# Norms four tiles ahead, Q of chunk 0 before K(4), and weight loads regrouped over two queues, in a linear-attention plus SwiGLU block

## The chip, the cores and the metric

The kernel runs on one core of a Trainium2 chip. Times are device microseconds (us) of one execution. A time in the tables is the median of a kernel's runs; the span of a profile, from its first to its last instruction, is about 1.7 us shorter than the time of the same execution. "Profile" and "trace" are the hardware profiler's record of one execution.

The engines are called as the profile calls them: PE is TensorE (matmuls), PEld its weight loads, DVE VectorE, ACT ScalarE, POOL GpSimd, SP SyncE. The kernel runs alone, so there is no second core to disturb it. A run more than 1.5% above the fastest of its kernel in the batch is counted as slow, and ratios leave it out.

## The reference, cut to what matters

```python
x = A_x                                   # 1 x 2048 x 512, bf16
xn = _layernorm(x, axis=-1)
return x + _A_ref(xn, A_wqkv, A_wo) + _B_ref(xn, B_w_gate, B_w_up, B_w_down)

# _A_ref: linear attention, 32 heads of 16
phi = lambda t: jnp.where(t > 0, t + 1, jnp.exp(t)) + 1e-6
pq, pk = phi(q), phi(k)
kv  = einsum("bhsd,bhse->bhde", pk, v);  z = einsum("bhsd->bhd", pk)
o   = einsum("bhqd,bhde->bhqe", pq, kv) / (einsum("bhqd,bhd->bhq", pq, z)[..., None] + 1e-6)
# _B_ref: (silu(xn @ w_gate) * (xn @ w_up)) @ w_down, inner width 1792
```

## The kernel before: the parts that matter

There are 16 tiles of 128 rows of x. For each tile t: VectorE computes the statistics (`bn1`, `bn2`), ScalarE the reciprocal root (`rs`: Ln, then Exp), and VectorE (tiles 0 to 3) or GpSimd (tiles 4 to 15) normalises. The normalised tile must be transposed. Tiles 0 to 3 go through PE and an eviction; the others go through a DMA transpose issued on the SyncE queue. Then PE computes K(t) of the tile, Q products (`qproj(i)`, four for each chunk of four tiles), and the accumulation `gacc(t)`. Every K or Q product ends in a chain over one of four PSUM banks (`phi`): exp on ScalarE, min on GpSimd, max-and-add on VectorE. This is the first stage, up to about 53 us. After it come 56 pairs of gate and up products, with the rest of the attention between them.

Each engine runs its own list in program order. A program-order list means that an instruction that is ready can still stand behind one that is not.

```python
        K.add("act", lambda e: e.preload_act_table_set("natural_log_exp_and_others"))
        xload("sp", 0)
        xload("act", 1)
        wload("sp", 1)          # K weights, 512 KB
        xload("act", 2)
        xload("sp", 3)
        xload("act", 4)
        wload("sp", 0)          # Q weights
        ...
        def norm(t):
            bn1(t)
            bn2(t)
            rs(t)
            lna_pool(t)
            dmat(t)             # DMA transpose, SyncE queue
            for piece in PIECES[t]:
                piece()         # weight loads of 448 to 896 KB, behind the transpose of tile 6, 7, ... 15
        ...
        for s in range(4, NT + 2):
            ends = []
            if s < NT:
                ends.append(kproj(s))
            for i in SQ[s]:
                ends.append(qproj(i))
            gacc(s - 2)
            if s + 3 < NT:
                norm(s + 3)     # three tiles ahead
            for e_ in ends:
                e_()
```

## Time and profile before

| | before |
|---|---|
| time, median of the first 3 runs | 224.49 us |
| span of the profiled execution | 222.1 us |
| PE busy | 213.5 us (96%) |
| end of the fourth K product (start of the first Q product) | 12.93 us |
| first gate matmul | 53.04 us |

The page of the profile gives busy time and count for each engine, a digit of busy tenths for each fortieth of the span, and the share of each engine in the chain of work that ended last. These are three of its lines from the kernel before.

```profile
PE 213.5 (96%) x1063; PEld 96.6 (43%) x1063; DVE 101.5 (46%) x171; ACT 70.2 (32%) x138; POOL 35.9 (16%) x81
...
PE   7599979999999999999999999999999999999995
...
PE 90%; ACT 3%; DMA 3%; DVE 2%; issue 0%; POOL 0%
```

PE is the limit, and its gaps are in the first third. The timeline of PE shows them one by one. Columns: start us, duration us, engine, source line, operation, tiles, count, and in brackets the idle time before it with what ended it. L219 is the warm-up (matmuls on zeros), L255 the PE transposes, L293 the K products, L302 the Q products, L309 `gacc`, L396 the gate and up products, L429 the z sum.

```profile
1.26 4.02 PE L219 MATMUL pb<-warm 128*128 128x512 bf16 x9 [1.26 <-DVE warm L197]
5.33 0.61 PE L255 MATMUL pb<-ident,xn 128*128 128x128 bf16 x4
7.06 0.40 PE L255 MATMUL pb<-ident,xn 128*128 128x128 bf16 x4 [1.13 <-DVE xn L237]
7.30 1.03 PE L293 MATMUL pb<-wqkv,xnT 128*128 128x512 bf16 x4
...
12.93 1.89 PE L302 MATMUL pb<-xnT,wqkv 128*128 128x512 bf16 x8
...
23.95 1.02 PE L293 MATMUL pb<-wqkv,xnT 128*128 128x512 bf16 x4 [0.50 <-DMA xnT<-xn]
...
33.19 1.02 PE L293 MATMUL pb<-wqkv,xnT 128*128 128x512 bf16 x4 [1.31 <-DVE pqT L287]
...
53.04 1.03 PE L396 MATMUL pb<-xnT,wg 128*128 128x512 bf16 x4
...
55.42 1.05 PE L429 MATMUL pb<-pk,ones 128*32 128x512 bf16 x16 [0.49 <-ACT GT L412]
```

Two things are to be read here. A group of four 128x512 matmuls takes 1.03 us in this view, with the drain of the last one; the next group starts 0.864 us after it, which is 0.216 us a matmul. The wait before K(10), at 33.19 us, is put down to VectorE, but VectorE had long freed the bank (at 29.62 us, after K(8)); the DMA transpose of tile 10, issued at 28.22 us, took 4.8 us to land, and this fits the start of K(10).

### The profile page before, as it was taken

What the parts mean: (1) busy time and instruction counts of PE and PEld (TensorE: products, weight loads), DVE (VectorE), ACT (ScalarE), POOL (GpSimd) and SP (SyncE); (2) the same over time, 40 slices, a digit from 0 to 9 for tenths busy, and PEclk for the clock granted to TensorE, in tenths of its full rate; (3) what the DMA queues carried; (4) which work ended last, traced back from release to release, by engine and by line L of the source; (5) the groups of instructions that cost most, each with busy time, mean ns of one, the idle gap of its engine ahead of it and who ended that gap; (6) DMA issues with size and microseconds to landing.
All of it is one profiled execution on the core that took longest, in us unless ns stands there. A gap on an engine that the chain in (4) does not pass through costs nothing.

```text
span 222.1 us, 2756 instructions
## 1 busy us (share of the span) xinstructions
PE 213.5 (96%) x1063; PEld 96.6 (43%) x1063; DVE 101.5 (46%) x171; ACT 70.2 (32%) x138; POOL 35.9 (16%) x81
## 2 busy tenths in 40 slices
PE   7599979999999999999999999999999999999995
PEld 2244334443544444444444444444444444444454
DVE  4598786655566777723223232422424232232121
ACT  3675555767372233313102131311313220130000
POOL 4187785843022000000000000000000000000000
DMA  6915999894000000000000000000000000000101
GB/s 204 351 36 134 255 183 234 224 270 152 0 0 3 0 0 0 3 0 24 24 0 27 24 0 0 24 24 2 25 24 0 3 24 0 25 24 3 47 24 47
DMA packets 16381, 13.55 MB, mean 61 GB/s; under 512 B 7280, under 2 KB 15344, under 8 KB 16368
## 3 DMA queue, kind: packets, MB, share of 16 engines
q1 hardware_dynamic: 15792, 12.85, 20.7%
q10 hardware_dynamic: 576, 0.52, 0.7%
q8 instruction: 8, 0.13, 0.3%
q14 instruction: 5, 0.04, 0.1%
HBM read 9.70 MB, written 2.10 MB: 53 GB/s over the span
## 4 chain that ended last, share of the span: by engine, by line
PE 90%; ACT 3%; DMA 3%; DVE 2%; issue 0%; POOL 0%
PE pb L396 43%; PE pb L492 22%; PE pb L488 6%; PE pb L302 6%; PE pb L293 5%; PE pb L309 5%; DMA xnT<-xn 1%; DMA x_sb<-in_A_x_dram 1%; PE pb L475 1%; ACT ef L283 1%; DVE xn L237 1%; PE pb L255 1%; ACT xnT L262 1%; ACT L400 1%; DVE stats L224 1%
## 5 line engine op out<-in xcount | busy, mean ns | idle before, releaser
L400 ACT ACTIVATE sil<-pb 128x512 bf16<-128x512 f32 x56 | 33.4, 597 | 106.0 <-PE pb L396 100.2
L405 DVE TENSOR_TENSOR hT<-pb,sil 128x512 bf16<-128x512 f32 x56 | 38.6, 688 | 46.9 <-PE pb L396 46.9
L396 PE MATMUL pb<-xnT,wg 128*128 128x512 bf16 x224 | 57.6, 379 | 0.0
L396 PE MATMUL pb<-xnT,wu 128*128 128x512 bf16 x224 | 57.5, 379 | 0.0
L492 PE MATMUL pb<-wd,hT 128*128 128x512 bf16 (+1 forms) x238 | 51.2, 366 | 0.0
L492 PEld LDWEIGHTS pb<-wd,hT 128*128 128x128 bf16 x238 | 23.3, 98 | 25.1
L498 DVE TENSOR_TENSOR out_sb<-pb,x_sb 128x512 bf16<-128x512 f32 (+1 forms) x17 | 11.2, 661 | 49.9 <-PE pb L492 49.9
L396 PEld LDWEIGHTS pb<-xnT,wu 128*128 128x128 bf16 x224 | 21.9, 98 | 26.4
L396 PEld LDWEIGHTS pb<-xnT,wg 128*128 128x128 bf16 x224 | 21.4, 98 | 27.3 <-issue 2.5
L283 ACT ACTIVATE ef<-pb 128x512 bf16<-128x512 f32 x32 | 19.0, 595 | 15.0 <-PE pb L293 9.9
L284 POOL TENSOR_SCALAR ef<-ef 128x512 bf16<-128x512 bf16 x32 | 19.6, 614 | 17.3 <-ACT ef L283 16.7
L293 PE MATMUL pb<-wqkv,xnT 128*128 128x512 bf16 x64 | 16.3, 379 | 1.8 <-DVE pqT L287 1.3
L488 PE MATMUL pb<-M,pqT 128*128 128x512 bf16 (+1 forms) x68 | 16.6, 366 | 0.0
L309 PE MATMUL pb<-pk,xn 128*128 128x512 bf16 x64 | 16.3, 379 | 0.0
L302 PE MATMUL pb<-xnT,wqkv 128*128 128x512 bf16 x64 | 16.1, 379 | 0.0
L287 DVE SCALAR_TENSOR_TENSOR pk<-pb,ef 128x512 bf16<-128x512 f32 x16 | 11.0, 686 | 7.8 <-POOL ef L284 7.8
L287 DVE SCALAR_TENSOR_TENSOR pqT<-pb,ef 128x512 bf16<-128x512 f32 x16 | 11.0, 691 | 4.2 <-POOL ef L284 4.1
L224 DVE BATCH_NORM_STATS2 stats<-x_sb 128x6 f32<-128x512 bf16 x16 | 10.9, 682 | 2.1 <-DMA x_sb<-in_A_x_dram 2.1
L483 DVE TENSOR_TENSOR pqT<-pb,pqT 128x512 bf16<-128x512 f32 x16 | 10.6, 681 | 0.0
L293 PEld LDWEIGHTS pb<-wqkv,xnT 128*128 128x128 bf16 x64 | 5.9, 98 | 9.2 <-DVE pqT L287 1.8
L488 PEld LDWEIGHTS pb<-M,pqT 128*128 128x128 bf16 x68 | 6.7, 98 | 7.4
L245 POOL TENSOR_SCALAR xn<-x_sb,nm,rstd 128x512 bf16<-128x512 bf16 x12 | 9.3, 772 | 2.0 <-ACT rstd L233 1.0
(61 smaller groups left out, 72.5 us busy)
## 6 DMA issues: line engine op xcount, KB each, us to landing
out_dram<-out_sb SPq DMA_DIRECT2D x15, 128.0 KB, 1.7
wg<-in_B_w_gate_dram SPq DMA_DIRECT2D x4, 448.0 KB, 5.1
wu<-in_B_w_up_dram SPq DMA_DIRECT2D x4, 448.0 KB, 3.8
wd<-in_B_w_down_dram SPq DMA_DIRECT2D x2, 896.0 KB, 7.4
x_sb<-in_A_x_dram SPq DMA_DIRECT2D x12, 128.0 KB, 5.1
wqkv<-in_A_wqkv_dram SPq DMA_DIRECT2D x3, 512.0 KB, 4.4
x_sb<-in_A_x_dram ACTq DMA_DIRECT2D x4, 128.0 KB, 4.5
wo<-in_A_wo_dram SPq DMA_DIRECT2D x1, 512.0 KB, 3.8
```

The source lines that it names most:

```text
L224: K.add("dve", lambda e: e.bn_stats(stats[:, t, :], x_sb[:, t, :]), r=[("x", t)], w=[("st", t)])
L283: K.add("act", lambda e: e.activation(buf, banks[b][:, :], ACT.Exp), r=[B(b)], w=[bkey])
L284: K.add("pool", lambda e: e.tensor_scalar(out=buf, in0=buf, scalar1=1.0 + 1e-6, scalar2=0.0, op0=ALU.min, op1=ALU.max), r=[bkey], w=[bkey])
L287: return lambda: K.add("dve", lambda e: e.scalar_tensor_tensor(out=dst, in0=banks[b][:, :], scalar=1e-6, in1=buf, op0=ALU.max, op1=ALU.add ...
L293: K.add("pe", [(lambda e, c=c: e.matmul(banks[b][:, :], xnT[:, c, t * P:(t + 1) * P], wqkv[:, c, D:2 * D], start=(c == 0), stop=(c == NDC ...
L302: K.add("pe", [(lambda e, c=c: e.matmul(banks[b][:, :], wqkv[:, c, g * P:(g + 1) * P], xnT[:, c, C * 512:(C + 1) * 512], start=(c == 0), s ...
L309: K.add("pe", [(lambda e, c=c: e.matmul(banks[c][:, :], xn[:, t, c * P:(c + 1) * P], pk[:, t, :], start=(t == 0), stop=(t == NT - 1))) for ...
L396: K.add("pe", [(lambda e, c=c, b=b, w_=w_: e.matmul(banks[b][:, :], w_[:, c, fc * P:(fc + 1) * P], xnT[:, c, C * 512:(C + 1) * 512], start ...
L400: K.add("act", lambda e: e.activation(sil[:, j % 2, :], banks[gb(j)][:, :], ACT.Silu), r=[B(gb(j))], w=[("sil", j % 2)])
L405: K.add("dve", lambda e: e.tensor_tensor(out=hT[:, C % 2, fc, :], in0=banks[gb(j) + 1][:, :], in1=sil[:, j % 2, :], op=ALU.mult), r=[B(gb( ...
L488: fns = [(lambda e, g=g: e.matmul(banks[bank][:, 0:hi - lo], pqT[:, g, t * P:(t + 1) * P], M[:, g, lo:hi], start=(g == 0), stop=False)) fo ...
L492: fns = [(lambda e, fc=fc: e.matmul(banks[bank][:, 0:hi - lo], hT[:, C % 2, fc, jj * P:(jj + 1) * P], wd[:, fc, lo:hi], start=False, stop= ...
```

## The change

The intent is to close those gaps. It has six parts:

1. x(0) is loaded in two column halves, one on each queue. x(1) thereby becomes the second load on the scalar queue.
2. K products run between the transposes, and evictions on ScalarE come ahead of exps.
3. The four Q products of chunk 0 come before K(4), and norms run four tiles ahead.
4. The first halves of the gate and up weights, the V weights and the output weights are loaded from the scalar queue between exps.
5. The second halves of gate and up, and the down weights, are loaded behind the last transpose.
6. The evictions of the G accumulators come ahead of the first silu, the z sum follows the second gate/up pair, and the denominator moves from after pair 2 to after pair 4 (the pairs are counted from 0).

The diff, cut to its core:

```diff
-        xload("sp", 0)
+        for h, eng in ((0, "sp"), (1, "act")):
+            load(eng, ("x", 0, h), x_sb[:, 0, h * 256:h * 256 + 256], xin[0:P, h * 256:h * 256 + 256])
         xload("act", 1)
         wload("sp", 1)
...
-        transp(0, 0, 0, 2)
-        transp(0, 1, 2, 4)
-        evac(0, 0, "act", 0, 2)
+        transp(0, 0)
         bn2(1)
-        evac(0, 1, "dve", 2, 4)
         rs(1)
-        lna_dve(1)
-        transp(1, 2)
-        evac(1, 2)
+        evac(0, 0)
         bn1(2)
         bn2(2)
         rs(2)
-        k0 = kproj(0)
+        lna_dve(1)
+        transp(1, 1)
+        evac(1, 1)
...
         norm(5)
+        k0()
+        q0 = qproj(0)
         k1()
-        q0 = qproj(0)
+        norm(6)
+        q1 = qproj(1)
         k2()
-        q1 = qproj(1)
+        k3()
         gacc(0)
...
+        AL = {4: lambda: fload("act", "wg", wg, B_w_gate, 0), 6: lambda: fload("act", "wu", wu, B_w_up, 0),
+              8: lambda: wload("act", 2), 10: lambda: woload("act")}
         for s in range(4, NT + 2):
...
-            if s + 3 < NT:
-                norm(s + 3)
+            if s + 4 < NT:
+                norm(s + 4)
+            if s in AL:
+                AL[s]()
...
+        for h in (1,):
+            fload("sp", "wg", wg, B_w_gate, h)
+            fload("sp", "wu", wu, B_w_up, h)
+        for lo in WD_LO:
+            dload("sp", lo)
...
+            elif j == 4:
+                den_mm()
+                hop(j)
+                recip(0)
+                recip(1)
+            elif j == 5:
+                hop(j)
                 recip(2)
                 recip(3)
-            elif j in (6, 9, 12, 15):
-                g = (j - 6) // 3
+            elif j in (7, 10, 13, 16):
+                g = (j - 7) // 3
                 bc_mm(g)
```

More of the change, by code (lines that the diff above doesn't have):

```diff
@@ L169, in wload, with woload, fload, dload @@
                  A_wqkv[:, i * D:(i + 1) * D].rearrange("(c p) f -> p c f", p=P))
-        def rload(key, dst, src, lo, hi):
-            load("sp", (key, lo), dst[:, lo:hi, :], src[lo * P:hi * P, :].rearrange("(c p) f -> p c f", p=P))
-        WD_LO = (0, 7)
-        PIECES = {t: [] for t in range(4, NT)}
-        PIECES[6].append(lambda: wload("sp", 2))
-        PIECES[7].append(lambda: rload("wo", wo, A_wo, 0, 4))
-        for c in range(NDC):
-            PIECES[8 + c].append(lambda c=c: rload("wg", wg, B_w_gate, c, c + 1))
-            PIECES[12 + c].append(lambda c=c: rload("wu", wu, B_w_up, c, c + 1))
-        for lo in WD_LO:
-            PIECES[15].append(lambda lo=lo: rload("wd", wd, B_w_down, lo, lo + 7))
+        def woload(eng):
+            load(eng, ("wo", 0), wo[:, :, :], A_wo.rearrange("(c p) f -> p c f", p=P))
+        FH = F // 2
+        def fload(eng, key, dst, src, h):
+            load(eng, (key, h), dst[:, :, h * FH:(h + 1) * FH],
+                 src[:, h * FH:(h + 1) * FH].rearrange("(c p) f -> p c f", p=P))
+        WD_LO = (0, 7)
+        def dload(eng, lo):
+            load(eng, ("wd", lo), wd[:, lo:lo + 7, :],
+                 B_w_down[lo * P:(lo + 7) * P, :].rearrange("(c p) f -> p c f", p=P))
         K.add("act", lambda e: e.preload_act_table_set("natural_log_exp_and_others"))
-        xload("sp", 0)
+        for h, eng in ((0, "sp"), (1, "act")):
+            load(eng, ("x", 0, h), x_sb[:, 0, h * 256:h * 256 + 256], xin[0:P, h * 256:h * 256 + 256])
         xload("act", 1)
@@ L220, in bass_parallel_sum__linear_attn_block__swiglu_ffn__prompt_kernel, with xk @@
                      for _ in range(NWARM)], r=[("warm",)], w=[B(0)])
+        def xk(t):
+            return [("x", t)] if t else [("x", 0, 0), ("x", 0, 1)]
         def bn1(t):
-            K.add("dve", lambda e: e.bn_stats(stats[:, t, :], x_sb[:, t, :]), r=[("x", t)], w=[("st", t)])
+            K.add("dve", lambda e: e.bn_stats(stats[:, t, :], x_sb[:, t, :]), r=xk(t), w=[("st", t)])
         def bn2(t):
@@ L238, in lna_dve @@
                 out=xn[:, t, :], in0=x_sb[:, t, :], scalar1=mv[:, t, 0:1], scalar2=rstd[:, t:t + 1],
-                op0=ALU.subtract, op1=ALU.mult), r=[("x", t), ("mv", t), ("rs", t)], w=[("xn", t)])
+                op0=ALU.subtract, op1=ALU.mult), r=xk(t) + [("mv", t), ("rs", t)], w=[("xn", t)])
         def lna_pool(t):
@@ L246, in lna_pool @@
                 out=xn[:, t, :], in0=x_sb[:, t, :], scalar1=nm[:, t:t + 1], scalar2=rstd[:, t:t + 1],
-                op0=ALU.add, op1=ALU.mult), r=[("x", t), ("nm", t), ("rs", t)], w=[("xn", t)])
+                op0=ALU.add, op1=ALU.mult), r=xk(t) + [("nm", t), ("rs", t)], w=[("xn", t)])
         def tview(b, n):
@@ L289, in phi, with kproj @@
                 r=[B(b), bkey], w=[dkey])
-        def kproj(t):
+        def kproj(t, late=False):
             b = nextbank()
@@ L296, in kproj @@
                 r=xkeys(t) + [("wqkv", 1)], w=[B(b)])
+            if late:
+                return lambda: phi(b, pk[:, t, :], ("pk", t))
             return phi(b, pk[:, t, :], ("pk", t))
@@ L325, in norm @@
             dmat(t)
-            for piece in PIECES[t]:
-                piece()
         bn1(0)
@@ L345, in bass_parallel_sum__linear_attn_block__swiglu_ffn__prompt_kernel @@
         rs(2)
-        k0 = kproj(0)
+        lna_dve(1)
+        transp(1, 1)
+        evac(1, 1)
         bn1(3)
-        lna_dve(2)
-        transp(2, 3)
-        evac(2, 3)
         bn2(3)
         rs(3)
-        k1 = kproj(1)
+        k0 = kproj(0, late=True)
+        lna_dve(2)
+        transp(2, 2)
+        evac(2, 2)
+        k0 = k0()
         lna_dve(3)
-        transp(3, 0)
-        evac(3, 0)
+        k1 = kproj(1, late=True)
+        transp(3, 3)
+        evac(3, 3)
+        k1 = k1()
         norm(4)
         k2 = kproj(2)
-        k0()
         k3 = kproj(3)
         norm(5)
-        k1()
-        q0 = qproj(0)
+        k0()
+        q0 = qproj(0)
+        k1()
+        norm(6)
+        q1 = qproj(1)
         k2()
-        q1 = qproj(1)
+        k3()
         gacc(0)
-        norm(6)
-        k3()
+        q2 = qproj(2)
         q0()
         gacc(1)
+        norm(7)
         q1()
-        SQ = {4: [2], 5: [3], 6: [], 16: [13, 14], 17: [15]}
+        q3 = qproj(3)
+        q2()
+        ends = [q3]
+        SQ = {4: [], 5: [], 6: [], 16: [13, 14], 17: [15]}
         for s in range(7, 16):
             SQ[s] = [s - 3]
+        AL = {4: lambda: fload("act", "wg", wg, B_w_gate, 0), 6: lambda: fload("act", "wu", wu, B_w_up, 0),
+              8: lambda: wload("act", 2), 10: lambda: woload("act")}
         for s in range(4, NT + 2):
-            ends = []
+            prev, ends = ends, []
             if s < NT:
                 ends.append(kproj(s))
+            for e_ in prev:
+                e_()
             for i in SQ[s]:
@@ L381, in bass_parallel_sum__linear_attn_block__swiglu_ffn__prompt_kernel @@
             gacc(s - 2)
-            if s + 3 < NT:
-                norm(s + 3)
-            for e_ in ends:
-                e_()
+            if s + 4 < NT:
+                norm(s + 4)
+            if s in AL:
+                AL[s]()
+            if s > 12:
+                for e_ in ends:
+                    e_()
+                ends = []
             if 12 <= s <= 15:
                 eb_copy(s - 12)
+        for h in (1,):
[3 more added lines that the diff above has]
+            dload("sp", lo)
         def gb(j):
@@ L398, in gu @@
                     start=(c == 0), stop=(c == NDC - 1))) for c in range(NDC)],
-                    r=sum([xkeys(t) for t in range(4 * C, 4 * C + 4)], []) + [(key, c) for c in range(NDC)], w=[B(b)])
+                    r=sum([xkeys(t) for t in range(4 * C, 4 * C + 4)], []) + [(key, fc // 7)], w=[B(b)])
             K.add("act", lambda e: e.activation(sil[:, j % 2, :], banks[gb(j)][:, :], ACT.Silu),
@@ L499, in oout @@
                 out=out_sb[:, t % 2, lo:hi], in0=banks[bank][:, 0:hi - lo], in1=x_sb[:, t, lo:hi], op=ALU.add),
-                r=[B(bank), ("x", t)], w=[("ob", t % 2, lo)])
+                r=[B(bank)] + xk(t), w=[("ob", t % 2, lo)])
             K.add("sp", lambda e: e.dma_start(oview[t * P:(t + 1) * P, lo:hi], out_sb[:, t % 2, lo:hi]),
@@ L507, in otile @@
             oout(b, t, 0, D)
+        gt_evac(1, "act")
+        gt_evac(0, "dve")
+        gt_evac(2, "act")
+        gt_evac(3, "dve")
         for j in range(NGU):
@@ L512, in bass_parallel_sum__linear_attn_block__swiglu_ffn__prompt_kernel @@
             if j == 0:
-                gt_evac(1, "act")
-                gt_evac(0, "dve")
-                gt_evac(2, "act")
-                gt_evac(3, "dve")
-                z_sum()
                 hop(j)
             elif j == 1:
+                z_sum()
                 kv_mm()
                 hop(j)
+            elif j == 2:
                 z_mm()
-            elif j == 2:
+                hop(j)
                 m_mm(0)
                 m_mm(1)
-                hop(j)
-                den_mm()
-                recip(0)
-                recip(1)
             elif j == 3:
@@ L533, in bass_parallel_sum__linear_attn_block__swiglu_ffn__prompt_kernel @@
                 hop(j)
+            elif j == 4:
[4 more added lines that the diff above has]
+            elif j == 5:
+                hop(j)
                 recip(2)
                 recip(3)
-            elif j in (6, 9, 12, 15):
-                g = (j - 6) // 3
+            elif j in (7, 10, 13, 16):
+                g = (j - 7) // 3
                 bc_mm(g)
@@ L542, in bass_parallel_sum__linear_attn_block__swiglu_ffn__prompt_kernel @@
                 hop(j)
-                if j in (7, 10, 13, 16):
-                    pqn((j - 7) // 3, 1)
-                    pqn((j - 7) // 3, 2)
                 if j in (8, 11, 14, 17):
-                    pqn((j - 8) // 3, 3)
+                    pqn((j - 8) // 3, 1)
+                    pqn((j - 8) // 3, 2)
+                if j in (9, 12, 15, 18):
+                    pqn((j - 9) // 3, 3)
             if C >= 1 and fc in O_SLOT:
```

## The prediction

> **What bounds the kernel.** TensorE. The page gives PE 213.5 of 222.1 us busy; the chain of waits is 90% PE. At its pace (four 128x512 matmuls every 0.864 us) only gaps can go. The timeline of PE shows them: about 3.3 us in the head (5.3 to 11.2 us), between PE transposes and the first K products; 0.5-0.65 us at 23.3 us (the transposed tile 7 lands late); 1.3-1.5 us at 31.7 us, before K(10); 0.5-0.65 us at 54.8 us, before the z sum. After that, none until the last output. The change can win about 5 us (2.2%), less what it adds.
>
> **Steps, costed with durations of the trace.**
> 1. Head. K products now run between transposes, and evictions on ScalarE precede exps. Walking the engines by hand (bn_stats 0.69, its aggregate 0.18, Ln+Exp 0.52, normalise 0.41, eviction 0.60), the fourth K product ends near 11.8 us, before 12.9: -1.2 us. It would be -2, but x(1) is now second on the scalar queue, issued together with the 512 KB of K weights. x(2), which stood so, landed at 5.5 us, as late as those weights (5.7). The Trainium skill ("DMA: Bandwidth & Descriptors", Queues, rings and completion order) says that engines go round-robin between queues by packets; the trace shows no head start for the small load. So I expect x(1) near 5.0 us instead of 3.5. Its bn_stats stands ahead of the normalisation of tile 0, so the first transpose moves from 5.3 to about 6.2 us.
> 2. Q of chunk 0 ahead of K(4). Eight exp-min-add chains and four norms follow closely; GpSimd (0.61 per min, 0.96 per norm) needs 8.7 us for them. Bank waits, about 0.5 us before accumulation 4.
> 3. Norms a step (2.6 us) earlier. K(10) waits for its DMA transpose, which took 4.8 us behind a 448 KB weight piece, against 2.4 undisturbed. A step more removes this wait and that at 23 us: -2. But the first half of the gate weights (896 KB, issued near 22 us on ScalarE, about 0.6 us there) lands ahead of the transpose of tile 8: one new wait of 0.5-1 us at K(8). Steps 1 to 3 together: K(10) starts near 31.6 instead of 33.2 us, -1.6.
> 4. GT evictions ahead of the activation table load (1.28 us), z sum after the second gate/up pair: -0.65.
> 5. The denominator moves from after pair 2 to after pair 4, its first use from after pair 6 to after pair 7. Den 0.69, four reciprocals in two lots of 1.75 with products between, and rhi/rlo take about 6.9 us from the den matmuls' start; PE arrives after 6.3: a new wait, +0.6.
> 6. Second weight halves (needed near 70 us) and down weights (95 us), issued near 40 us, about 3.6 MB at 230-350 GB/s, are in time: 0.
>
> Sum: -1.6 - 0.65 + 0.6, about -1.7 on 224.4.
>
> **Prediction:** 222.7 us, 8 in 10 within 220.6 to 224.6. Faster by over 2%: 0.08; within 2%: 0.90; slower by over 2%: 0.02.
>
> **What would show it.** First transpose later than 5.8 us with VectorE waiting on x_sb (1); fourth K product near 11.8 us; no wait at K(10), one on xnT at K(8) (3); none at the z sum (4); 0.4-0.8 us before the first reciprocal broadcast near 71 us (5); none before gate block 7 or down (6).
>
> **What would make it wrong.** x(1) landing by 4.2 us: another -0.8. Transposes on a queue of their own not held up by weight loads: -0.7 more. ScalarE stalling in issuing 896 KB loads, or GpSimd's backlog holding banks through the early stages: up to +2.

## The result and the profile after

| | before | after |
|---|---|---|
| time, median of 4 runs | 224.29 us | 225.28 us (225.01 to 225.45) |
| ratio | | 1.0051 (95%: 1.0027 to 1.0075) |
| span of the profiled execution | 222.1 us | 223.7 us |
| end of the fourth K product | 12.93 us | 14.19 us |
| from there to the first gate matmul | 40.11 us | 40.63 us |
| from there to the end | 169.06 us | 168.88 us |

A ratio in this document is the mean time of one kernel's fast runs over that of the other kernel's fast runs of the same rounds, so it is not quite the ratio of the medians quoted beside it. One of the four runs of before (227.41 us) counts as slow and is not in it. The time is the same within 2%, and slightly but clearly slower. It lies outside my range (220.6 to 224.6), on the slow side.

In the profiled executions the head lost 1.26 us (14.19 - 12.93), the rest of the first stage 0.52 us, and the second stage won 0.18 us. The work that PE does in each of the three parts is the same in both kernels.

The timeline of PE after the change, at the same places. L222 is the warm-up, L261 the transposes, L299 the K products, L310 the Q products, L317 `gacc`, L454 the z sum, L500 the first broadcast of the reciprocals, L421 the gate and up products.

```profile
1.26 3.94 PE L222 MATMUL pb<-warm 128*128 128x512 bf16 x9 [1.26 <-DVE warm L200]
7.21 0.40 PE L261 MATMUL pb<-ident,xn 128*128 128x128 bf16 x4 [2.00 <-DVE xn L243]
8.39 0.61 PE L261 MATMUL pb<-ident,xn 128*128 128x128 bf16 x4 [0.79 <-DVE xn L243]
8.79 1.91 PE L299 MATMUL pb<-wqkv,xnT 128*128 128x512 bf16 x4
...
14.19 2.08 PE L310 MATMUL pb<-xnT,wqkv 128*128 128x512 bf16 x8
...
24.21 1.04 PE L317 MATMUL pb<-pk,xn 128*128 128x512 bf16 x4 [0.17 <-DVE pk L293]
25.45 1.04 PE L299 MATMUL pb<-wqkv,xnT 128*128 128x512 bf16 x4 [0.20 <-DMA xnT<-xn]
...
29.78 1.04 PE L299 MATMUL pb<-wqkv,xnT 128*128 128x512 bf16 x4 [1.57 <-DMA xnT<-xn]
...
54.82 1.03 PE L421 MATMUL pb<-xnT,wg 128*128 128x512 bf16 x4
...
58.37 1.05 PE L454 MATMUL pb<-pk,ones 128*32 128x512 bf16 x16
...
73.55 0.40 PE L500 MATMUL pb<-rhi,Eb 32*128 32x512 bf16 x4 [0.38 <-POOL rlo L487]
```

The wait of 2.0 us before the first transpose was foreseen, though shorter. What was not foreseen is the line at 8.79 us: four matmuls in 1.91 us instead of 1.03. PE was back at half speed. The table of stretches of the changed kernel shows it too. Columns: the stretch, its length, busy us of PE, PEld, DVE, ACT and POOL, then the granted clock, the busy share of the DMA engines, and GB/s.

```profile
5.00:8.41 3.41, 0.62 (x6) 0.25 (x6) 2.23 (x7) 1.10 (x4) 0.00 (x0) 1.00 1.10 365
8.41:11.82 3.41, 3.41 (x15) 1.76 (x16) 2.71 (x7) 1.90 (x7) 0.00 (x0) 0.50 1.11 349
```

In the first stretch PE is busy for 0.62 of 3.41 us. The clock of the second is 0.50, and PE counts as busy for all of it. In the kernel before, every stretch that I asked for shows clock 1.00, even that of the warm-up matmuls, which took 0.43 us each; a1 tells why this can't be taken at its word.

The first cause is a load. The timeline of DVE (same columns) shows the statistics of x(0), those of x(1), and the normalisation of tile 0, first before the change:

```profile
3.35 0.69 DVE L224 BATCH_NORM_STATS2 stats<-x_sb 128x6 f32<-128x512 bf16 x1 [2.15 <-DMA x_sb<-in_A_x_dram]
...
4.18 0.66 DVE L224 BATCH_NORM_STATS2 stats<-x_sb 128x6 f32<-128x512 bf16 x1
4.86 0.41 DVE L237 TENSOR_SCALAR xn<-x_sb,mv,rstd 128x512 bf16<-128x512 bf16 x1
```

and after it:

```profile
3.09 0.69 DVE L230 BATCH_NORM_STATS2 stats<-x_sb 128x6 f32<-128x512 bf16 x1 [1.88 <-DMA x_sb<-in_A_x_dram]
...
6.14 0.69 DVE L230 BATCH_NORM_STATS2 stats<-x_sb 128x6 f32<-128x512 bf16 x1 [2.15 <-DMA x_sb<-in_A_x_dram]
6.75 0.40 DVE L243 TENSOR_SCALAR xn<-x_sb,mv,rstd 128x512 bf16<-128x512 bf16 x1
```

x(0) came 0.26 us earlier than before (3.09 against 3.35 us). x(1) came at 6.14 us; before, its statistics had begun at 4.18 us without any wait. Tile 0 had its reciprocal root at 4.56 us, but its normalisation stands behind the statistics of x(1) in VectorE's list, and so waited until 6.75 us. The DMA issues of a short stretch around 1.4 us (queue, count, size, us from issue to landing) show with what x(1) was issued.

```profile
wqkv<-in_A_wqkv_dram SPq DMA_DIRECT2D x1, 512.0 KB, 5.1
x_sb<-in_A_x_dram ACTq DMA_DIRECT2D x1, 128.0 KB, 4.9
```

The 128 KB of x(1) landed at the time of the 512 KB of the K weights. The Trainium skill's page "DMA: Bandwidth & Descriptors", in its section Issuing engines are not separate DMA queues, says that DMAs from different engines run on the same 16 DMA engines and interleave, and that issuing from several engines saves only the sequencer's time. The two lines agree: the small load landed 0.2 us before the large one and not well ahead of it. Sharing is not the whole of it, though: from 2.75 to 4.0 us, with both loads issued, the DMA engines moved only 29 GB/s, against 261 GB/s in the kernel before and 252 GB/s in a2. What held them back there is not shown. Splitting x(0) gained a quarter of a microsecond on x(0) and pushed x(1) into the company of the largest early load.

The chain of waits of the changed kernel, in order of time (start us, us, what), gives the second large wait.

```profile
25.12 4.62 DMA xnT<-xn
...
29.78 1.04 PE pb L299 x4
```

The transpose of tile 8 was ready to be issued at 25.12 us, 1.2 us after ScalarE had issued the 896 KB of gate weights, and it took 4.62 us to land instead of the 2.4 us of the undisturbed ones. K(8) started 1.7 us later than PE could have (28.05 us).

### The profile page after: what moved, and what is told of

Read it like the earlier page. It is cut to its first block, busy times and chain, and to the rows that moved or that the text cites. A ratio compares the mean times of both kernels' runs of the same rounds, so it can differ in the third digit from the quotient of the medians.

```text
span 223.7 us, 2733 instructions
## 1 busy us (share of the span) xinstructions
PE 213.8 (96%) x1043; PEld 97.3 (43%) x1063; DVE 101.2 (45%) x170; ACT 70.0 (31%) x138; POOL 35.7 (16%) x81
## 4 chain that ended last, share of the span: by engine, by line
PE 85%; DMA 4%; POOL 4%; DVE 3%; issue 1%; ACT 1%; POOLq 0%
PE pb L421 41%; PE pb L517 22%; PE pb L513 6%; PE pb L299 4%; PE pb L310 4%; PE pb L317 4%; DMA x_sb<-in_A_x_dram 2%; DMA xnT<-xn 2%; POOL xn L251 2%; POOL ef L290 2%; PE pb L500 1%; DVE rd L485 1%; DVE stats L230 1%; PE pb L261 1%; PE pb L476 0%
## 5 line engine op out<-in xcount | busy, mean ns | idle before, releaser
L421 PE MATMUL pb<-xnT,wg 128*128 128x512 bf16 x221 | 57.0, 379 | 0.3 <-issue 0.2
L421 PE MATMUL pb<-xnT,wu 128*128 128x512 bf16 x216 | 55.9, 379 | 0.4
L421 PEld LDWEIGHTS pb<-xnT,wu 128*128 128x128 bf16 x224 | 21.9, 98 | 26.4
L421 PEld LDWEIGHTS pb<-xnT,wg 128*128 128x128 bf16 x224 | 21.5, 98 | 27.1 <-issue 2.1
L299 PE MATMUL pb<-wqkv,xnT 128*128 128x512 bf16 x63 | 17.4, 404 | 1.8 <-DMA xnT<-xn 1.8
L317 PE MATMUL pb<-pk,xn 128*128 128x512 bf16 x62 | 16.2, 379 | 0.3 <-DVE pk L293 0.2
L310 PE MATMUL pb<-xnT,wqkv 128*128 128x512 bf16 x63 | 16.2, 379 | 0.1
L508 DVE TENSOR_TENSOR pqT<-pb,pqT 128x512 bf16<-128x512 f32 x16 | 10.6, 681 | 0.2 <-PE pb L500 0.2
L299 PEld LDWEIGHTS pb<-wqkv,xnT 128*128 128x128 bf16 x64 | 6.3, 104 | 9.8 <-DMA xnT<-xn 2.8
L317 PEld LDWEIGHTS pb<-pk,xn 128*128 128x128 bf16 x64 | 6.2, 98 | 8.0 <-DVE pk L293 0.7
```

The costliest lines, as they stand in the source:

```text
L299: K.add("pe", [(lambda e, c=c: e.matmul(banks[b][:, :], xnT[:, c, t * P:(t + 1) * P], wqkv[:, c, D:2 * D], start=(c == 0), stop=(c == NDC ...
L310: K.add("pe", [(lambda e, c=c: e.matmul(banks[b][:, :], wqkv[:, c, g * P:(g + 1) * P], xnT[:, c, C * 512:(C + 1) * 512], start=(c == 0), s ...
L317: K.add("pe", [(lambda e, c=c: e.matmul(banks[c][:, :], xn[:, t, c * P:(c + 1) * P], pk[:, t, :], start=(t == 0), stop=(t == NT - 1))) for ...
L421: K.add("pe", [(lambda e, c=c, b=b, w_=w_: e.matmul(banks[b][:, :], w_[:, c, fc * P:(fc + 1) * P], xnT[:, c, C * 512:(C + 1) * 512], start ...
```

## The experiments

Twelve kernels were run, in four batches on four chips (a1 to a4; b1, b2, b4 and b5; c1 to c3; c4). Each came out correct, each was timed beside runs of the kernel before, and those runs of before had medians of 224.2 to 224.3 us in every batch. The changed kernel was not timed again in these batches, so a difference to it, or between kernels of two batches, is one of medians from different rounds; the ratios to before are the safer figures. In the first theory the changed kernel loses by three separate things: the late x(1), the half clock that follows it, and weight loads ahead of transposes. The main rival is that the new order itself loses.

### a1: x(0) whole again

```diff
-        for h, eng in ((0, "sp"), (1, "act")):
-            load(eng, ("x", 0, h), x_sb[:, 0, h * 256:h * 256 + 256], xin[0:P, h * 256:h * 256 + 256])
+        xload("sp", 0)
```

> The changed kernel with x(0) loaded whole on the SyncE queue again, so that x(1) is the first load on the scalar queue as before. Theory 1 (the head is lost because x(1) lands late, at 6.1 us, and TensorE then runs at half clock until 11.8 us): x(1) lands near 3.5 us, first transpose at 5.3 us, no matmul at 0.43 us spacing, fourth K product ends near 11.0 us instead of 14.2, wait at K(8) stays at 1 to 2 us; time 2.5 to 3.3 us below the changed kernel, near 222.3. Rival (the new order of the head itself, K products between transposes and late exps, costs the time): the first transpose comes early but the fourth K product still ends at 12.9 us or later, and less than 1.5 us is won.

Measured: median 223.69 us, ratio to before 0.9932 (0.9879 to 0.9985). x(1) came early, and the statistics of x(1) started at 4.15 us. The first transpose was at 5.30 us as expected. The wait at K(8) stayed, with 1.2 us. The half clock stayed too in the profiled execution, as the timeline of PE shows (L260 transposes, L298 K products, L309 Q products), though the table of stretches calls it full (last line).

```profile
5.30 0.61 PE L260 MATMUL pb<-ident,xn 128*128 128x128 bf16 x4
6.97 0.61 PE L260 MATMUL pb<-ident,xn 128*128 128x128 bf16 x4 [1.07 <-DVE xn L242]
7.37 1.91 PE L298 MATMUL pb<-wqkv,xnT 128*128 128x512 bf16 x4
...
12.85 2.07 PE L309 MATMUL pb<-xnT,wqkv 128*128 128x512 bf16 x8
...
7.37:10.70 3.33, 3.33 (x14) 1.50 (x13) 2.58 (x8) 1.93 (x5) 0.00 (x0) 1.00 1.11 350
```

The fourth K product therefore ended at 12.85 us, not at 11.0. But the six runs fall into two groups: 221.65 and 221.84 us, with a mean granted clock of 1.000, and 223.64 to 224.10 us, of which three have a clock of 0.992. (The fourth, the profiled one, has 1.000 in its record although its matmuls ran at half speed. The first entry of its clock record is a rise to full clock at 10.58 us, and the view shows 1.00 for what lies before the first entry. The spacing of the matmuls misses nothing.) By the medians 1.6 us were won, less than I expected, and with 12.85 us my rival's sign was nearly met. But the timeline shows the half clock in the place of that time, and a3 and b2 test it.

So my account of the half clock as a consequence of the late x(1) alone is wrong. In this execution PE did not cool down in the gap of 1.07 us: it had not been at full speed at all before 10.58 us.

The clock records show more than I read from them. Ten of the fourteen profiles have one, and up to the last matmul their changes lie whole multiples of 3.41 us apart. What PE did in one such step goes with the clock of the next. Six times a full clock was followed by a half one, and in the step before PE was busy for 18 to 50% of it (18% in the changed kernel, 41% in b1, 50% in c2). After steps with 75 and 76% (b2, c3) the clock stayed full. A half clock became full only after steps with 84% or more, and not after 68% (a1, whose 4.02 us of warm-up fell across two steps) or 76% (c2). Where the steps begin differs: the warm-up started at 1.25 or 1.26 us in all ten, the first rise came at 4.1 to 10.6 us. So one and the same gap can cost nothing in one execution and 3.4 us at half speed in another. These shares are read from the traces; no run was made to test them.

### a2: the K weights issued after x(3)

```diff
-        wload("sp", 1)
         xload("act", 2)
         xload("sp", 3)
+        wload("sp", 1)
```

> The changed kernel with x(0) still in two column halves, but the K weights issued after x(3) on the SyncE queue, so that x(1) has no 512 KB beside it. If x(1) was late because it shares the engines with the K weights issued in the same half microsecond: x(1) lands near 3.5 to 4.2 us, the K weights near 6.3, and the head gains 2 us or more. If it is late because of the halves themselves (512 byte rows, after which the DMA engines move under 60 GB/s from 2.75 to 4.0 us): that hole stays and x(1) lands at 4.8 us or later.

Measured: median 223.96 us, ratio 0.9968 (0.9925 to 1.0012). x(0) was still in halves, and the statistics of x(1) started at 4.16 us. So it is the place beside the K weights that delayed x(1). The head gained only 0.93 us (fourth K product 13.26 us), because x(2) now stood beside the K weights: its statistics waited until 6.19 us, PE idled 1.83 us before the transposes of tile 1, and the K products ran at half clock (1.50 and 1.91 us).

### a3: thirteen warm-up matmuls

```diff
-NWARM = 9
+NWARM = 13
```

> The changed kernel with 13 warm-up matmuls instead of 9: TensorE stays busy until about 6.9 us, x(1) is still late. Measures the clock by itself. Theory 1: the half-clock stretch (8.5 to 11.8 us) is due to the idle 2.0 us before the first transpose: all K products at 0.216 us spacing, mean granted clock 1.000, fourth K product ends near 13.0 us instead of 14.2, 1.0 to 1.3 us won in time. Rival (the clock falls with no relation to that gap, or costs nothing because VectorE and ScalarE set the pace of the head): half-clock matmuls stay, or under 0.4 us won.

Measured: median 223.22 us, ratio 0.9951 (0.9904 to 0.9998), 2.1 us below the median of the changed kernel. x(1) was as late as before (6.16 us). The warm-up ended at 6.83 us, and every K product ran at full clock. The timeline of PE:

```profile
7.22 0.40 PE L261 MATMUL pb<-ident,xn 128*128 128x128 bf16 x4 [0.40 <-DVE xn L243]
8.40 0.40 PE L261 MATMUL pb<-ident,xn 128*128 128x128 bf16 x4 [0.78 <-DVE xn L243]
8.64 1.03 PE L299 MATMUL pb<-wqkv,xnT 128*128 128x512 bf16 x4
...
12.57 1.03 PE L310 MATMUL pb<-xnT,wqkv 128*128 128x512 bf16 x4
```

The first transposes stand where they stood in the changed kernel (7.21 us), and the fourth K product ends at 12.57 instead of 14.19 us. With the load unchanged and useless work added, 1.6 us of the head came back (and 1.3 us of the time of the two profiled executions). This settles that the half clock is a cost of its own, and that keeping PE busy removes it.

### a4: all later weights behind the last transpose

```diff
-        AL = {4: lambda: fload("act", "wg", wg, B_w_gate, 0), 6: lambda: fload("act", "wu", wu, B_w_up, 0),
-              8: lambda: wload("act", 2), 10: lambda: woload("act")}
+        AL = {}
...
+        fload("sp", "wg", wg, B_w_gate, 0)
+        fload("sp", "wu", wu, B_w_up, 0)
+        wload("sp", 2)
+        woload("sp")
         for h in (1,):
```

> The changed kernel with all weight loads after the first Q and K ones (first halves of gate and up, V weights, output weights) moved from the scalar queue to the SyncE queue, behind the last transpose. Theory 2 (the transpose of tile 8 is late because the 896 KB gate load issued at 23.95 us is ahead of it on the DMA engines): every DMA transpose lands in 2.4 to 2.6 us, waits at K(7) (0.4 us) and K(8) (1.7 us) gone, 1.7 to 2.1 us won, head unchanged at 14.2 us; the gate weights land near 47, up near 50 us, before their use at 52.5. Rival (tile 8 is late because GpSimd and VectorE normalise it late, backlog of Q before K(4)): the wait stays above 1 us with undisturbed transposes.

Measured: median 223.19 us, ratio 0.992 (0.9872 to 0.9968), 2.1 us below the changed kernel. The wait before K(8) is gone, and the weights were in time. Time from issue to landing of the transposes (min, median, max), first in the changed kernel:

```profile
DMA to landing us min/median/max: 2.4/3.1/5.5
```

and in a4:

```profile
DMA to landing us min/median/max: 2.4/2.4/4.0
```

This rules out the rival that tile 8 was normalised too late. One part missed: a transpose of 4.0 us remained, that of tile 7, those of tiles 9 and 11 took 3.2 and 3.6 us, and K(7) still waited 0.34 us. The head happened to be different too (x(1) at 5.36 us, half clock until 13.3 us, the fourth K product ended at 14.63), so this run says nothing of the head.

### b5: x(0) in row halves

```diff
-            load(eng, ("x", 0, h), x_sb[:, 0, h * 256:h * 256 + 256], xin[0:P, h * 256:h * 256 + 256])
+            load(eng, ("x", 0, h), x_sb[h * 64:h * 64 + 64, 0, :], xin[h * 64:h * 64 + 64, :])
```

> The changed kernel with x(0) in two row halves (64 rows of 1024 bytes) instead of two column halves (128 rows of 512 bytes), one on each queue as before, x(1) still second on the scalar queue beside the K weights. If x(1) is late by its place beside the K weights: it lands at 5.2 us or later and the time is that of the changed kernel within 0.7 us. If the short rows of the column halves hold up the DMA engines: x(1) lands near 4 us and 1.5 us or more is won.

Measured: median 226.11 us, ratio 1.0084 (1.0033 to 1.0134). The statistics of x(1) started at 6.43 us. The median is 0.8 us above that of the changed kernel, a little more than the 0.7 that I allowed, but from another batch. So the short rows of the column halves are not the cause; the place of x(1) is.

### b1: x(0) whole, weights last, denominator after pair 3

The kernel of a1 with the edit of a4, and this:

```diff
                 m_mm(3)
+                den_mm()
                 hop(j)
-            elif j == 4:
-                den_mm()
-                hop(j)
                 recip(0)
                 recip(1)
-            elif j == 5:
+            elif j == 4:
                 hop(j)
```

> The changed kernel with x(0) whole, all later weights behind the last transpose, and the denominator one pair earlier (after pair 3, first use after pair 7 as in the changed kernel). If the three costs are separate and add: waits at K(8) (1.2 us in the run with x(0) whole) and before the first broadcast (0.55 us) gone, the half-clock stretch from 5.3 to 10.7 us still there in most executions: 221.7 us, about 2 us below the run with x(0) whole alone. If the weights in one block behind the last transpose come too late for the first gate/up pair or V weights, a new wait stands between 51 and 60 us and less than 1.2 us is won.

Measured: median 222.81 us, ratio 0.991 (0.9866 to 0.9953), and not the 221.7 expected. The waits at K(8) and at the broadcast were gone, but the list of waits has a new one of my own making (L478 is the denominator, L497 the eviction of M).

```profile
PE pb L478 <- ACT M L497: 1.0, 1, 1.0
```

The denominator writes PSUM bank 2, and the M product just ahead of it had filled that bank. Again two groups of runs: 221.03 and 221.07 us at clock 1.000, and 223.04 to 223.25 us at clock 0.992, with 222.58 us between. They are 2 us apart, as in a1.

### b2: three matmuls in the gap

The kernel of b1, and this:

```diff
         transp(0, 0)
+        K.add("pe", [(lambda e: e.matmul(banks[7][:, :], warm[:, 0:P], warm[:, :], start=True, stop=True))
+                     for _ in range(3)], r=[("warm",)], w=[B(7)])
```

> The kernel of b1_x0_last_den with three more warm-up matmuls between the transposes of tile 0 and of tile 1, where TensorE idled 1.07 us. If the half clock comes from that gap: no K product at 0.43 us spacing, the fourth K product ends near 11.3 us instead of 12.9, about 1.2 us below b1_x0_last_den, near 220.5, and a smaller spread between executions. If the clock does not depend on it: K products stay at 0.43 us and it is the same as b1_x0_last_den or 0.3 us slower.

Measured: median 221.39 us, ratio 0.9869 (0.9831 to 0.9907), every run at clock 1.000. The three matmuls filled the gap at half clock (1.29 us), and the next ones were at full clock.

```profile
5.71 1.29 PE L340 MATMUL pb<-warm 128*128 128x512 bf16 x3
7.37 0.40 PE L260 MATMUL pb<-ident,xn 128*128 128x128 bf16 x4 [0.36 <-DVE xn L242]
7.65 1.02 PE L298 MATMUL pb<-wqkv,xnT 128*128 128x512 bf16 x4
```

It won 1.4 us by the medians, 0.7 us by the means (222.34 and 221.60), since b1 is at full clock in some of its runs anyway. The fourth K product ended at 12.22 us, not at 11.3: the second K product waited for tile 2.

### b4: the kernel before with the weights last

The kernel before, with the pieces taken out of `norm`, gate and up in column halves, and all these loads issued on the SyncE queue once the last transpose is issued.

```diff
-            for piece in PIECES[t]:
-                piece()
...
+            if s == 12:
+                fload("wg", wg, B_w_gate, 0)
+                fload("wu", wu, B_w_up, 0)
+                wload("sp", 2)
+                ...
```

> The kernel before with nothing changed but the weight loads from V weights on: gate and up in column halves, all on the SyncE queue behind the last transpose. If the waits at tile 7 (0.65 us) and K(10) (1.5 us) in the kernel before come from weight pieces ahead of the transposes, as I read them, they go without norms running a step earlier: 222.2 us, 2 us won, every transpose landing in 2.4 to 3.2 us. If the transposes were late for want of the earlier norms, the waits stay and it is the same as before.

Measured: median 222.69 us, ratio 0.9927 (0.989 to 0.9964), 1.5 us below the median of before in the same rounds. One edit to the kernel before wins what the whole change lost and more, without any norm moving. The waits at tile 7 and K(10) went; one of 0.83 us appeared at K(9). The profiled execution also ran at half clock in the head, from 9.3 to 12.7 us, which the profile of before did not. So the kernel before is exposed to it as well. In this kernel no weight is loaded in the stretch 27 to 29 us, and yet the transpose of tile 9 took 4.1 us. The issues and queues of two short stretches there, 27 to 28 and 28 to 29 us:

```profile
xnT<-xn SPq DMA_TRANSPOSE x1, 4.1
...
q8 instruction: 1, 0.02, 6.7%
```

An instruction fetch stands beside it. In a4, b1, b2, c1 and c2 the transpose of 3.9 to 4.1 us also was under way when the one q8 fetch of that part of the trace came. The packets say more than the coincidence in time. In c1 all packets but seven of the transpose of tile 7 had started by 21.3 us; the seven start from 21.99 us on, as the fetch ends (21.04 to 22.00 us). All ten profiles in which the fetch met just one transpose show the same, with two to seven last packets (in five of them a weight load was issued meanwhile). And in c4 the fetch met none. So a wait behind the fetch is well supported, though I could not move the fetch by itself. In the kernel before, the slow transpose of tile 10 had both a 448 KB piece and such a fetch beside it, so how much of that wait was due to which stays open.

### c3: the kernel before with the three matmuls

```diff
         transp(0, 1, 2, 4)
+        K.add("pe", [(lambda e: e.matmul(banks[7][:, :], warm[:, 0:P], warm[:, :], start=True, stop=True))
+                     for _ in range(3)], r=[("warm",)], w=[B(7)])
```

> The kernel before with three warm-up matmuls added after the transposes of tile 0, where TensorE idles 1.13 us. The profile of before shows full clock from 7.0 us on, but one of its variants (b4) had K products at 0.43 us there. If the half clock also strikes some executions of before: the spread between executions shrinks and the mean falls by 0.3 to 1.0 us, nothing falls below 222.9. If before is never affected: the same within 0.3 us.

Measured: median 224.04 us, ratio 0.997 (0.9933 to 1.0006): the same. The profile was at full clock, but so was that of before. Five of its six runs were fast, all at clock 1.000; one, of 227.3 us, was counted as slow and is left out. Its profiled execution had a wait of 2.0 us at K(8). How often the half clock strikes it, the record tells in part: of the 44 runs of before timed beside the experiments, 17 list a clock of 0.992 or less (one step of 3.4 us at half speed is 0.8% of the span). Their median is 224.48 us, that of the other 27 is 224.22 us. As a1 shows, a listed 1.000 does not exclude a half clock at the start. So far as this goes, the clock costs the kernel before little.

### c1: the best version

The kernel of b2 with the denominator mended:

```diff
             elif j == 3:
-                m_mm(2)
-                m_mm(3)
+                den_mm()
                 hop(j)
-            elif j == 4:
-                den_mm()
-                hop(j)
                 recip(0)
                 recip(1)
-            elif j == 5:
+            elif j == 4:
+                m_mm(2)
+                m_mm(3)
                 hop(j)
```

(against the changed kernel.)

> The kernel of b2_filler with the mistake in my earlier denominator mended: there its matmuls wanted the bank that the last M product had just filled, and waited 0.96 us for ScalarE to empty it. Now the denominator takes the place of the last two M products after pair 3, and they come after pair 4. If that wait was the bank and nothing else: no wait between 50 us and the end, neither at the denominator nor at the broadcast, 0.96 us below b2_filler: near 220.5 us, over 1.5% below the kernel before. If the denominator chain is still too late for the first broadcast: a wait of up to 0.5 us there.

Measured: median 220.51 us (220.18 to 220.93), as expected, ratio to before 0.9819 (0.9786 to 0.9851). The interval lies well below 1, but the gain of 1.8% is not clear of 2%. It has the lowest median, and the smallest spread of the kernels with six runs. This is its whole list of PE waits:

```profile
PE pb L221 <- DVE warm L199: 1.3, 1, 1.3
PE pb L260 <- DVE xn L242: 0.7, 1, 0.7
PE pb L298 <- DMA xnT<-xn: 0.2, 1, 0.2
```

The fourth K product ended at 11.91 us, the first gate matmul came at 50.77 us, and the span was 219.2 us. The three parts of the result's table are 11.91, 38.86 and 168.43 us. Waits of this list leave out the few tenths that PE loses between two groups without idling; the 44 products of the middle part need 44 x 0.864 = 38.0 us.

### c2: the same with the K weights after x(3)

```diff
-        wload("sp", 1)
         xload("act", 2)
         xload("sp", 3)
+        wload("sp", 1)
```

> The kernel of c1_best with the K weights issued after x(3) instead of before it. In b2_filler the second and third K products waited for tile 2, whose x(2) stood beside the K weights. If that place is what delays a tile: x(2) lands near 4.3 instead of 5.6 us, the wait of 0.5 us before the transposes of tile 2 goes, the K weights still land by 7.5 us, and it is 0.3 to 0.6 us below c1_best. If the K weights become the last to arrive: the first K product starts later than 7.65 us and nothing is won.

Measured: median 224.2 us, with five runs from 224.05 to 224.44 and one of 220.13 us. The five are counted as slow because they are over 1.5% above the fastest, so no ratio is given, and I use the profile (of a slow run) only to say what happened in it. The transposes of tile 1 came early, at 6.53 us, but the K weights landed only at 8.98 us.

```profile
9.12 1.86 PE L298 MATMUL pb<-wqkv,xnT 128*128 128x512 bf16 x4 [2.19 <-DMA wqkv<-in_A_wqkv_dram]
```

PE idled for 2.19 us and then ran at half clock. The rival of my expectation holds in this execution. It also shows how narrow the head is: two executions of this one kernel are 4 us apart.

### c4: the best version with norms three ahead

```diff
-        norm(7)
...
-            if s + 4 < NT:
-                norm(s + 4)
+            if s + 3 < NT:
+                norm(s + 3)
```

> The kernel of c1_best with the norms three tiles ahead again, as in the kernel before, everything else kept. Tells what the fourth tile of lead is worth once no weight load stands before a transpose. If the loads were the main cause of late transposes: waits of 0.4 to 0.9 us at one or two K products (a single transpose of 4 us still turns up in every profile without loads, beside an instruction fetch), 220.5 to 221.5 us. If the lead itself is what hides the transposes: waits at several K products and 222 us or more.

Measured: median 221.4 us, ratio to before 0.9874 (0.9839 to 0.9909), every run at clock 1.000. The lead of a fourth tile is worth 0.9 us by the medians, though c1 ran on another chip and the intervals of the two ratios just overlap. In the profile one wait of 1.66 us stands before K(7), and the part from the fourth K product to the first gate matmul takes 40.00 us (10.72 to 50.72), 1.1 us more than in c1.

```profile
23.09 1.04 PE L298 MATMUL pb<-wqkv,xnT 128*128 128x512 bf16 x4 [1.66 <-DMA xnT<-xn]
```

That transpose was not slow: it was issued late, at 20.66 us, and took 2.4 us. No transpose of c4 was slow, against my expectation of one of 4 us; its q8 fetch (19.49 to 20.42 us) fell between two of them. Time from issue to landing of all twelve (min, median, max), first in c1, then in c4:

```profile
DMA to landing us min/median/max: 2.4/2.4/3.9
...
DMA to landing us min/median/max: 2.4/2.4/2.5
```

The head of c4 has the code of c1's, and yet it ended at 10.72 us instead of 11.91: x(2), issued together with the K weights in both, landed at 5.27 us in c4 and at 6.46 us in c1.

## Why the prediction was wrong, point by point

I predicted -1.7 us on 224.4 us. The runs measured a ratio of 1.0051, which is +1.1 us; the two profiles differ by +1.6 us. Of the parts, in the profiled executions:

| part | predicted | profiles |
|---|---|---|
| head, to the end of the fourth K product (step 1) | -1.2 | +1.26 |
| rest of the first stage (steps 2 and 3) | -0.4 | +0.52 |
| second stage (steps 4, 5, 6) | -0.05 | -0.18 |

(The -0.4 is what step 3 gave for all three steps together, -1.6, less the -1.2 of step 1.)

**Step 1 failed: "the fourth K product ends near 11.8 us, before 12.9: -1.2 us".** It ended at 14.19 us. Two terms were wrong. In a3, where x(1) is as late but the clock is full, it ended at 12.57 us: of the 2.4 us missed, 1.6 are the clock's, and the other 0.8 go, by difference, with the late x(1).

- *The load of x(1).* The mechanism was right: it landed with the K weights (a2, b5), and the normalisation of tile 0 waited behind it. I wrote 5.0 us, half a microsecond before the landing of x(2), which stood in that place in the kernel before; the prediction does not say how. It was 6.1 us in the changed kernel and in a3, 6.4 in b5, and 5.4 in a4. The term was mis-sized by 0.4 to 1.4 us. I had read the trace against a rule, too. The Trainium skill's page "DMA: Bandwidth & Descriptors", section Queues, rings and completion order, says that an engine takes turns between queues by packets; taken simply, a small load on a queue of its own should soon be through. Neither kernel shows that.
- *The clock.* This term was missing altogether. I walked the engines with durations of a warm PE. The trace that I read had the evidence, warm-up matmuls at 0.43 us and first transposes at 0.61 us. The Trainium skill's page "TensorE: Matmul & The Clock Gate", Part 1, describes it: the clock of the array is halved or full according to how busy PE was in a free-running window of about 3.4 us, and the point of change differs between executions. The runs here agree: the clock entries of the traces lie multiples of 3.41 us apart, the half clock of the changed kernel lasts one such step (8.41 to 11.82), and runs of a1 and b1 fall into two groups 2 us apart. On one point they differ from the page, whose table speaks of an idle window: here a step in which PE was busy for 18% (the changed kernel) to 50% (c2) of it was enough. Nor does the gap alone decide: in the kernel before, after a gap of 1.13 us, PE was at full speed at 7.06 us; in a1, after 1.07 us, it was still at half speed at 6.97 us, because it had not yet reached full speed. Where the steps lie is chance, and this fits the page's free-running window. By a3 the clock cost 1.6 us of head and 2.1 us of time.

The order of the head itself does no harm: with x(0) whole and PE kept busy it ends at 11.91 us in the profile of c1 and at 10.72 us in that of c4. That 11.91 is close to the 11.8 us predicted is luck, since the landing of x(2) alone moves it by over 1 us.

**Step 2 held in place and size, not in kind.** "Bank waits, about 0.5 us before accumulation 4": `gacc(4)` started at 24.21 us, when PE could have started it at 23.87, so 0.34 us. But it waited for no bank. It waited for its input `pk` of tile 4, which VectorE finished at 24.15 us.

**Step 3 was right in kind and wrong in size.** The wait at K(10) went, and a new one came at K(8) behind the 896 KB gate load. I wrote 0.5 to 1 us; it was 1.7 us. The wait at K(7), which I wrote off, stayed with 0.38 us (25.07 to 25.45). Summed over K(10) (-1.5), K(7) (-0.3), K(8) (+1.7) and `gacc(4)` (+0.3), this is +0.3 of the +0.5 us; the rest is tenths between groups. a4 shows that the loads are the cause of the wait at K(8), and c4 that the lead of a fourth tile is worth 0.9 us once they are out of the way. b4 shows that moving the loads away is worth more, 1.5 us, in the kernel before. And the wait at K(10) in the kernel before, which I had put down to a weight piece, had an instruction fetch beside it that I had not looked for.

**Step 4 held.** The wait before the z sum shrank from 0.66 us (54.76 to 55.42) to 0.10 us: -0.56 against a predicted -0.65.

**Step 5 held.** "A new wait, +0.6": pair 7 ended at 73.00 us by the pace of its matmuls and the broadcast started at 73.55, so 0.55 us, ended by the last `rlo` on GpSimd. In c1, with the denominator one pair earlier, it is gone.

**Step 6 held.** No wait at gate block 7 or at the down products.

Among the things that would make me wrong, I had named stalls of ScalarE in issuing loads. They did not happen: the issue of 896 KB took 0.39 us there.

So the change did not fail by its idea. Mended, it is 1.8% faster than the kernel before (c1, with x(0) whole, PE kept busy, loads last and the denominator one pair earlier). Not all of that is its order's: the loads alone give 0.7% in the kernel before (b4), and the three matmuls 0.3% that is not clear of noise (c3). The 0.8 to 1.1% that are left for the order are an estimate from these ratios, and no run isolates them. As written the change pays this back in three places that are not the order: x(1) beside the K weights, PE falling to half clock while it waits for it, and a large load ahead of a transpose that PE needs soon. a1, a3 and a4 mend one of these each, and their medians lie 1.6 to 2.1 us below that of the changed kernel.

## What to carry to other kernels

When a load is split over two queues, follow what moves behind it: the load that slips by one place may be the one the engines wait for, and a small load issued together with a large one lands with the large one. Count the start of a kernel at the speed PE really has there: look at the spacing of the first matmuls, and fill gaps ahead of the first real products with matmuls on zeros until they run at full speed. Put weight loads behind the DMA transposes that feed the next products, if there is time to load them later at all.

## What the Trainium skill lacked or had wrong

- "TensorE: Matmul & The Clock Gate", Part 1, gives an idle window of about 3.4 us for the fall to half clock. Here a step of 3.41 us in which PE was busy for 0.62 us (the changed kernel), 1.39 us (b1) or 1.70 us (c2) was enough. Its rule for authors, no gaps over 3.4 us, is too mild: the gap of 2.0 us in the changed kernel was followed by a half clock that cost 2.1 us of time (a3), and b1 fell after gaps of 0.7 and 1.3 us. Further down, the page itself tells of a kernel whose clock swung because PE idled briefly but often between groups of matmuls; it gives no share of busy time as a limit.
- The same page warns that the clock events of a trace have been seen to be unreliable. It does not say that a trace can lack the half clock at its start, nor that the spacing of matmuls shows it. In the profile of a1 the clock is shown as 1.00 from 7.37 to 10.70 us, while four matmuls took 1.91 us there.
- "DMA: Bandwidth & Descriptors", Queues, rings and completion order, lets one expect that a small load on one queue is not held up for the length of a large one on another. Here 128 KB issued together with 512 KB landed 4.9 us after its issue, the large one 5.1 us after.
- No page that I read says what an instruction fetch costs a DMA transpose. In six kernels with no weight load near (a4, b1, b2, b4, c1, c2) one transpose of 3.9 to 4.1 us stands among others of mostly 2.4 us. It was under way during the only q8 fetch of that stretch (0.9 to 1.1 us), and its last packets start when the fetch ends. In c4 the fetch fell between two transposes, and none took over 2.5 us. No run moves the fetch alone.
